# Block 0 of a fused S4D and feed-forward kernel: VectorE's limit over four steps from 7.5 to 7.0

## The chip, the cores and the metric

The kernel runs on one core of one Trainium2 chip. The metric is the device time of one execution in microseconds (us); lower is better. Each core has TensorE (PE, with its weight loads PEld), VectorE (DVE), ScalarE (ACT), GpSimd (POOL) and SyncE (SP), each with its own instruction stream in a fixed order, and 16 DMA engines that serve the queues of SP, ACT and POOL.

## What is computed

One residual layer on 2048 tokens of 576 channels: a layer norm with modulation, a state space model as a long convolution (S4D), a second layer norm, and a feed-forward network of 4608 hidden units.

```python
def _A_ref(u, log_A_real, A_imag, C_real, C_imag, log_dt, D_skip):
    ...
    P = jnp.exp((A * dt[:, None])[:, :, None] * pos[None, None, :])
    K = 2.0 * jnp.einsum("dn,dnl->dl", C, P).real
    ...  # y = causal convolution of u with K, by FFT
    return y + u * D_skip[None, None, :]

def _B_ref(x, w1, w2):
    h = jnp.einsum("bsd,df->bsf", x, w1)
    return jnp.einsum("bsf,fd->bsd", jnp.maximum(h, 0), w2)

x = A_u
sa, ca, ga, sb, cb, gb = ...  # from silu(c) @ w_mod
h = _layernorm(x) * (1 + ca) + sa
x = x + ga * _A_ref(h, ...)
h = _layernorm(x) * (1 + cb) + sb
x = x + gb * _B_ref(h, B_w1, B_w2)
```

All is float32. Where a product is large, a factor is split into a high and a low part that TensorE takes in its faster float32 form, and three products are added (high by high, high by low, low by high).

## The kernel before

**Blocks and groups.** The tokens are cut into four blocks of 512. The feed-forward network of a block runs over 36 groups g of 128 hidden units, so groups 0 to 35 are block 0 and group 36 is the first of block 1. A group has an up-projection `first(g)`, 14 products into `hps` (line L1352), here called F0, F1 and so on, and a down-projection `second(g)`, 14 products into the accumulators `acc` (L1378), here S0, S1 and so on. The code emits F(g+1) ahead of S(g). Between them ScalarE writes the high part `hh` of the rectified result (L1357) and VectorE the low part `hl` (L1358), which needs `hh`; S(g) has nine products with `hh` and five with `hl`.

**Weights.** In block 0 each group's weights are loaded from HBM by SP into `r` (`r1` has two buffers, L1297; `r2` three, L1301), ScalarE rounds them to the high part in `w` (L1317 and L1327), and VectorE subtracts to get the low part (L1322; L1333 and L1334). These subtractions are the last readers of `r`, so a load into that buffer is released by VectorE. The low parts are stored (L1434) for the later blocks, which load them instead.

**What is handed out.** While a block's groups run, the work that the next block needs is handed out in small pieces by a generator: for block 0 this is `block0()`. It holds, in this order: the rest of the convolution's kernel (rotations on VectorE, L462 to L468, and small products `kps`, L496, of TensorE); the first norm of block 1's tokens (L893 to L928); and `conv(1)`, the convolution of block 1. That one has Fourier products `ps_f` (L844) with ScalarE's copies (L845), butterflies on VectorE (L858 to L872), multiplications of spectra of 128x1152 (L1038 to L1044), inverse products `ps_i` (L1065) which VectorE adds to the tokens (L1070), and at its end the activations of block 1: norm statistics (L893, L902, L906, L907, and L903 on ScalarE), scaled tokens `h` (L1166), transposes `ps_t` through one PSUM buffer (L1174), `xf` and its high part `xh` or `xs` on ScalarE (L1178, L1180), and the low part `xl` or `xs` on VectorE (L1183, L1185). F36 needs all of `xs`, `xh` and `xl`.

After S35 ScalarE copies the accumulators (`o`, `oT`, L1462 and L1467), a product `ps_o` (L1482) turns one of them, VectorE scales them and adds them to the tokens (L1487 to L1495), and POOL stores them (L1497). Then block 1 begins with six more rotations, for which POOL loads `W`, `Zr` and `W2r`; their buffers take the place of those of `conv(1)` and of block 0's results.

**The hand-out.** `step(g)` is called four times a group, 144 times a block. Each call draws pieces from the generator. A piece yields its estimated VectorE time in us, or None for a piece of TensorE's. A call stops when the work done has reached a target that grows by 2.15 per step in block 0, when this call has 2.7 us of VectorE's work or two pieces of TensorE's, or when VectorE's work over this call and the three before it reaches a limit, `room`. A piece can also yield -1, which ends the call. What is left after step 143 is emitted at once.

A list scheduler then orders each engine's instructions: it keeps most of the code's order but puts an instruction ahead where it reckons that the one in front must wait. So a piece that is handed out at another step moves rows on all engines.

Of the kernel before, what the change touches and what calls it, by code (L numbers as in the profile page):

```python
# [24 lines left out]
NF = F // P  # L25
# [522 lines left out]
class Body:  # L548
# [736 lines left out]
    def ffn(self, gens):  # L1285
# [53 lines left out]
        def first(g):  # L1339
            xh, xl, xs = self.xT[g // NF]  # L1340
            w = w1.pop(g)
            ps = self.fps.tile([P, 512], F32, tag="hps", bufs=2, name="hps")
            ops = [(w[:, 0, 4], xs), (w[:, 1, 4], xs)]
            if g:
                for k in range(4):
                    ops += [(w[:, 0, k], xh[:, k]), (w[:, 0, k], xl[:, k]), (w[:, 1, k], xh[:, k])]
            else:
                for k in range(4):
                    ops[2 * k : 2 * k] = [(w[:, 0, k], xh[:, k]), (w[:, 1, k], xh[:, k])]
                ops += [(w[:, 0, k], xl[:, k]) for k in range(4)]  # L1350
            for i, (a, x) in enumerate(ops):
                nc.tensor.matmul(ps, a, x, start=(i == 0), stop=(i == 13))  # L1352
                if i == 6:
                    step(g)
            hh = ff.tile([P, 512], F32R, tag="hh", bufs=2, name="hh")
            hl = ff.tile([P, 512], F32R, tag="hl", bufs=2, name="hl")
            nc.scalar.activation(hh, ps, AF.Relu)  # L1357
            nc.vector.scalar_tensor_tensor(hl, ps, 0.0, hh, op0=ALU.max, op1=ALU.subtract)  # L1358
            return hh, hl

        def second(g, hh, hl):
            f = g % NF
            if f == 0:
                self.acc = [
                    self.fps.tile([P, 512], F32, tag=f"acc{i}", name=f"acc{i}_{g}")
                    for i in range(5)
                ]
            acc, w = self.acc, w2.pop(g)
            tail = [(4, w[:, 512:640], hh), (4, w[:, 512:640], hl)]
            ops = []  # L1370
            for i in range(4):
                tk = slice(i * P, (i + 1) * P)
                ops += [(i, hh[:, tk], w[:, 0:512]), (i, hh[:, tk], w[:, 640:]), (i, hl[:, tk], w[:, 0:512])]
            ops = tail + ops if f == NF - 1 else ops + tail
            seen = [0] * 5
            for j, (i, a, x) in enumerate(ops):
                seen[i] += 1
                nc.tensor.matmul(  # L1378
                    acc[i], a, x,
                    start=(f == 0 and seen[i] == 1),  # L1380
                    stop=(f == NF - 1 and seen[i] == (3 if i < 4 else 2)),
                )
                if j == 6:
                    step(g)

        done, recent = [0.0], []

        def step(g):

            at[0] += 1  # L1390
            target = self.rate(g // NF) * (at[0] % 144 or 144)
            gen = gens[g // NF]
            v = pe = 0.0
            room = (7.5, 7.0, 7.0, 7.0)[g // NF] - sum(recent[-3:])
            recent.append(0.0)
            while done[0] < target and v < min(room, 2.7) and pe < 2:
                w = next(gen, 0)
                if gen.gi_frame is None or w == -1:
                    return
                if w is None:  # L1400
                    pe += 1
                    done[0] += (0.35, 0.7, 0.7, 0.7)[g // NF]
                else:
                    v += w
                    recent[-1] = v
                    done[0] += w
# [20 lines left out]
        for g in range(n + 1):  # L1427
            if g < n:
                if g + 3 < n:
                    load_r1(g + 3)  # L1430
                if g + 3 < n:
                    load_r2(g + 3)
                for dst, src in late:
                    nc.sync.dma_start(out=dst, in_=src.bitcast(F32))  # L1434
                late.clear()
                new = (g, *first(g))
                if g + 1 < n:
                    hi2(g + 1)
                    lo2(g + 1)
                if g + 2 < n:  # L1440
                    hi1(g + 2)
                    lo1(g + 2)
                if g + 3 < n:
                    low1(g + 3)
                step(g)
            if prev is not None:
                second(*prev)
                if prev[0] % NF == NF - 1:
                    self.evacuate(prev[0] // NF)
            if g < n:  # L1450
                prev = new
                step(g)
                if g % NF == NF - 1:
                    for _ in gens[g // NF]:
                        pass
                    done[0] = 0.0
# [126 lines left out]
```

## Time and profile before

| | |
|---|---|
| median of 3 runs (lowest to highest) | 1346.46 us (1346.43 to 1348.98) |
| the profiled execution's own time | 1348.05 us |
| its span, first to last instruction | 1346.3 us |
| TensorE, VectorE, ScalarE busy | 1236.1, 892.7, 496.9 us |
| mean granted TensorE clock | 0.952 |
| block 0's groups on TensorE, F0 to the end of S35 | 223.3 to 561.3 us |

All intervals in the text come from this one profiled execution. In a timeline row the columns are start and length in us, engine, line, operation, output<-inputs, shapes, count, and in brackets the engine's idle time before it with what ended it. In a row of the chain of waits they are start, length and what ran or was waited for. Products overlap, so their pitch is read from start to start. A wait that is named in the profile is put down to what came last.

### The profile page before, as it was taken

What the parts mean: (1) busy time and instruction counts of PE and PEld (TensorE: products, weight loads), DVE (VectorE), ACT (ScalarE), POOL (GpSimd) and SP (SyncE); (2) the same over time, 40 slices, a digit from 0 to 9 for tenths busy, and PEclk for the clock granted to TensorE, in tenths of its full rate; (3) what the DMA queues carried; (4) which work ended last, traced back from release to release, by engine and by line L of the source; (5) the groups of instructions that cost most, each with busy time, mean ns of one, the idle gap of its engine ahead of it and who ended that gap; (6) DMA issues with size and microseconds to landing.
All of it is one profiled execution on the core that took longest, in us unless ns stands there. A gap on an engine that the chain in (4) does not pass through costs nothing.

```text
span 1346.3 us, 26017 instructions
## 1 busy us (share of the span) xinstructions
PE 1236.1 (92%) x10720; PEld 983.0 (73%) x10720; DVE 892.7 (66%) x1324; ACT 496.9 (37%) x863; POOL 162.5 (12%) x260
## 2 busy tenths in 40 slices
PE   4566686899999998999999999999999999999997
PEld 2345564678777786777777887887888888888885
DVE  5889988899996899588458995457996221111112
ACT  5678523222223422622244225433323352323331
POOL 0657511011000100110001000100000000000000
PEclk9558788999999999999999999999999999999998
DMA  8557983889778976797778995877996567666651
GB/s 269 217 208 298 313 317 94 313 302 328 282 252 317 334 248 238 258 400 282 243 274 328 353 355 162 268 224 267 351 394 188 176 178 230 194 197 196 201 177 53
DMA packets 120843, 345.85 MB, mean 257 GB/s; under 512 B 23916, under 2 KB 24212, under 8 KB 109972
## 3 DMA queue, kind: packets, MB, share of 16 engines
q1 hardware_dynamic: 103828, 226.96, 51.1%
q0 software_dynamic: 16384, 115.85, 22.7%
q8 instruction: 84, 1.38, 0.4%
q10 hardware_dynamic: 512, 1.38, 0.3%
q14 instruction: 35, 0.29, 0.1%
HBM read 262.73 MB, written 81.40 MB: 256 GB/s over the span
## 4 chain that ended last, share of the span: by engine, by line
PE 82%; DVE 10%; DMA 3%; issue 2%; ACT 1%; POOL 1%; POOLq 0%; ACTq 0%; SPq 0%; DVEq 0%
PE acc L1378 32%; PE hps L1352 32%; PE kps L496 5%; PE ps_f L844 5%; PE kps L71 2%; PE ps_i L1065 2%; PE ph L71 2%; DMA r<-in_w_dram 2%; DVE W1r L464 1%; DVE T L62 1%; DVE T L462 1%; DMA Zr<-Zd 1%; DVE k L62 1%; PE ps_t L1174 1%; POOL W L68 1%
## 5 line engine op out<-in xcount | busy, mean ns | idle before, releaser
L1352 PE MATMUL hps<-xh,w 128*128 128x512 f32 x1152 | 388.2, 397 | 1.2 <-ACT xh L47 1.2
L1378 PE MATMUL acc<-w,hh 128*128 128x512 f32 x1152 | 368.0, 402 | 8.0 <-ACT hh L1357 8.0
L1358 DVE SCALAR_TENSOR_TENSOR hl<-hps,hh 128x512 fp32r<-128x512 f32 x144 | 99.0, 688 | 307.2 <-ACT hh L1357 306.4
L1378 PEld LDWEIGHTS acc<-w,hh 128*128 128x128 f32 x1152 | 216.7, 189 | 55.9 <-ACT hh L1357 9.3
L1352 PEld LDWEIGHTS hps<-xh,w 128*128 128x128 f32 x1152 | 215.4, 188 | 48.6 <-ACT xh L47 2.5
L1352 PE MATMUL hps<-xl,w 128*128 128x512 f32 x576 | 231.6, 402 | 0.7 <-DVE xl L47 0.5
L1378 PE MATMUL acc<-w,hl 128*128 128x512 f32 x576 | 224.9, 402 | 2.2 <-DVE hl L1358 2.2
L1357 ACT ACTIVATE hh<-hps 128x512 fp32r<-128x512 f32 x144 | 86.0, 598 | 296.1 <-PE hps L1352 291.7
L1327 ACT ACTIVATE w<-r 128x576 fp32r<-128x576 f32 x141 | 96.7, 686 | 240.9 <-PE acc L1378 233.6
L1378 PEld LDWEIGHTS acc<-w,hl 128*128 128x128 f32 x576 | 108.0, 189 | 26.6 <-DVE hl L1358 3.5
L1317 ACT ACTIVATE w<-r 128x640 fp32r<-128x640 f32 x140 | 102.6, 733 | 65.3 <-DMA r<-in_w_dram 57.0
L1352 PEld LDWEIGHTS hps<-xl,w 128*128 128x128 f32 x576 | 108.3, 188 | 25.1 <-DVE xl L47 1.7
L1352 PE MATMUL hps<-xs,w 128*128 128x512 f32 x288 | 96.7, 409 | 1.1 <-DVE w L1322 1.1
L71 PE MATMUL kps<-W,W 128*32 128x16 f32 x2304 | 45.1, 218 | 45.9 <-POOL W L68 28.6
L496 PEld LDWEIGHTS kps<-W1r,W2r 128*32 128x32 f32 x3456 | 67.8, 146 | 24.8 <-issue 15.2
L71 PEld LDWEIGHTS kps<-W,W 128*32 128x32 f32 x2304 | 40.4, 150 | 58.3 <-POOL W L68 31.1
L1044 DVE TENSOR_TENSOR Y<-Y,T 128x1152 f32<-128x1152 f32 x60 | 79.4, 1350 | 0.0
L496 PE MATMUL kps<-W1r,W2r 128*32 128x48 f32 (+2 forms) x3456 | 76.3, 238 | 1.9 <-PE hps L1352 1.0
L845 ACT ACTIVATE Z<-ps_f 128x288 f32<-128x288 f32 x120 | 48.9, 409 | 66.2 <-PE ps_f L844 64.9
L1497 POOL DMA_DIRECT2D out_dram<-x x16 | 8.7, 545 | 471.5 <-DVE x L1489 468.9
L1352 PEld LDWEIGHTS hps<-xs,w 128*128 128x128 f32 x288 | 53.4, 189 | 12.7 <-DVE w L1322 1.5
L1378 PE MATMUL acc<-hl,w 128*128 128x512 f32 x144 | 56.6, 393 | 0.0
(230 smaller groups left out, 1568.7 us busy)
## 6 DMA issues: line engine op xcount, KB each, us to landing
r<-in_w_dram SPq DMA_DIRECT2D x144, 320.0 KB, 6.6
r<-in_w_dram SPq DMA_DIRECT2D x144, 288.0 KB, 3.7
w<-L1d SPq DMA_DIRECT2D x108, 320.0 KB, 3.2
w<-L2d SPq DMA_DIRECT2D x108, 288.0 KB, 2.7
W2r<-W2d POOLq DMA_DIRECT2D x18, 1536.0 KB, 8.8
W2d<-W SPq DMA_DIRECT2D x12, 1536.0 KB, 8.6
Ua<-Ud POOLq DMA_DIRECT2D x15, 1152.0 KB, 9.5
W<-W1d POOLq DMA_DIRECT2D x18, 768.0 KB, 10.4
```

The source lines that it names most:

```text
L62: self.tc.keep_in_program_order(self.nc.vector.tensor_tensor(out, a, b, op=op))
L71: self.tc.keep_in_program_order(self.nc.tensor.matmul(*args, **kw))
L496: nc.tensor.matmul(ps[32 * dd : 32 * dd + 32, q, :], W2[:, r, :, ch], W1[:, :, r, ch], start=(r == 0), stop=(r == 1),)
L844: nc.tensor.matmul(o, fc[:, n2, c, :], src(n2), start=True, stop=True)
L845: ev = nc.scalar.activation(Z[:, n2, c], ps[:, :PC], AF.Copy)
L1044: v(y, y, T, op=op or ALU.add)
L1317: copy(g - 1)(w1[g][:, 0], r1[g], AF.Copy)
L1327: copy(g)(w[:, 0:D], r2[g], AF.Copy)
L1352: nc.tensor.matmul(ps, a, x, start=(i == 0), stop=(i == 13))
L1357: nc.scalar.activation(hh, ps, AF.Relu)
L1358: nc.vector.scalar_tensor_tensor(hl, ps, 0.0, hh, op0=ALU.max, op1=ALU.subtract)
L1378: nc.tensor.matmul(acc[i], a, x, start=(f == 0 and seen[i] == 1), stop=(f == NF - 1 and seen[i] == (3 if i < 4 else 2)),)
```

## The change

One number, in `step` inside `ffn`:

```diff
-            room = (7.5, 7.0, 7.0, 7.0)[g // NF] - sum(recent[-3:])
+            room = (7.0, 7.0, 7.0, 7.0)[g // NF] - sum(recent[-3:])
```

In block 0 the four-step window of VectorE's handed-out work closes 0.5 earlier. With 7.5 the hand-out follows the target over most of the block and has given out all by step 135; steps 136 to 143 draw nothing but waiting pieces. With 7.0 the window binds nearly everywhere, the work falls behind the target, and the last piece, the fifth transposed tile of block 1, is drawn at step 143. No instruction's kind, count or shape changes.

Three places show the move. First TensorE, where the last inverse product of block 1 stands. Before, it is followed by F34 (`w_6106`), a group and more before the block's last down-projection:

```order
L1065 MATMUL ps_i<-V_1_6107,gc 128x288 x2
L1352 MATMUL hps<-xs_2822,w_6106 128x512 x2
L1352 MATMUL hps<-xh_2820,w_6106 128x512
L1065 MATMUL ps_i<-V_1_6107,gc 128x288 x2
L1352 MATMUL hps<-xl_2821,w_6106 128x512
L1352 MATMUL hps<-xh_2820,w_6106 128x512 x2
L1352 MATMUL hps<-xl_2821,w_6106 128x512
```

After, it is the row of `ps_i` here, three products into S35 (`w_6265`), of which eleven are left:

```order
L1378 MATMUL acc_0_3039<-hh,w_6265 128x512
L1378 MATMUL acc_0_3039<-hl,w_6265 128x512
L1378 MATMUL acc_0_3035<-w_6265,hh 128x512
L1065 MATMUL ps_i<-V_1_6181,gc 128x288 x2
L1378 MATMUL acc_0_3035<-w_6265,hh 128x512
L1378 MATMUL acc_0_3035<-w_6265,hl 128x512
L1378 MATMUL acc_0_3036<-w_6265,hh 128x512 x2
L1378 MATMUL acc_0_3036<-w_6265,hl 128x512
```

The inverse product has moved from the front of F34 into the last down-projection of the block.

Second TensorE, where block 1's transposes stand. Before, they lie among products of S34 (`w_6270`) and F36 (`w_6276`), with S35 (`w_6357`) still to come:

```order
L1378 MATMUL acc_0_3040<-hh,w_6270 128x512
L1174 MATMUL ps_t<-ident,h_6248 128x128 x2
L1174 MATMUL ps_t<-ident,h_6249 128x128 x2
L1378 MATMUL acc_0_3040<-hl,w_6270 128x512
L1352 MATMUL hps<-xs_6153,w_6276 128x512 x2
L1352 MATMUL hps<-xh_6151,w_6276 128x512
L1174 MATMUL ps_t<-ident,h_6248 128x128 x2
L1174 MATMUL ps_t<-ident,h_6249 128x128 x2
L1352 MATMUL hps<-xl_6152,w_6276 128x512
L1352 MATMUL hps<-xh_6151,w_6276 128x512 x2
L1352 MATMUL hps<-xl_6152,w_6276 128x512
```

After, S35 is over when the first transposes come, and the products of F36 (`w_6202`) and F37 (`w_6270`) are mixed behind them; the remaining transposes stand between those:

```order
L1378 MATMUL acc_0_3038<-w_6265,hh 128x512 x2
L1378 MATMUL acc_0_3038<-w_6265,hl 128x512
L1174 MATMUL ps_t<-ident,h_6340 128x128 x2
L1174 MATMUL ps_t<-ident,h_6341 128x128 x2
L1174 MATMUL ps_t<-ident,h_6340 128x128 x2
L1174 MATMUL ps_t<-ident,h_6341 128x128 x2
L1352 MATMUL hps<-xs_6246,w_6202 128x512 x2
L1352 MATMUL hps<-xs_6246,w_6270 128x512 x2
L1174 MATMUL ps_t<-ident,h_6340 128x128 x2
L1174 MATMUL ps_t<-ident,h_6341 128x128 x2
L1352 MATMUL hps<-xh_6244,w_6202 128x512
```

All five tiles' transposes have moved behind S35, so no product of block 0 is left to run beside them.

Third VectorE, the multiplications of block 1's last spectrum with its second pair of factors, from one `hl` to the next. Before, seven of them lie between the `hl` of groups 30 and 31, and the eighth behind it:

```order
L1358 SCALAR_TENSOR_TENSOR hl<-hps,hh 128x512
L1042 TENSOR_TENSOR T<-Ka,Ua 128x1152
L1333 TENSOR_TENSOR w_6045<-r_5896,w_6045 128x64
L1044 TENSOR_TENSOR Y_1_5972<-Y_1_5972,T 128x4x288
L1334 TENSOR_TENSOR w_6045<-r_5896,w_6045 128x512
L1322 TENSOR_TENSOR w_5996<-r_5957,w_5996 128x640
L1042 TENSOR_TENSOR T<-Ka,Ua 128x1152 x2
L1044 TENSOR_TENSOR Y_1_5972<-Y_1_5972,T 128x4x288 x2
L1042 TENSOR_TENSOR T<-Ka,Ua 128x1152
L1358 SCALAR_TENSOR_TENSOR hl<-hps,hh 128x512
```

After, the gap between `hl` of group 32 and of group 33 holds eight of them:

```order
L1358 SCALAR_TENSOR_TENSOR hl<-hps,hh 128x512
L1042 TENSOR_TENSOR T<-Ka,Ua 128x1152 x2
L1044 TENSOR_TENSOR Y_1_6050<-Y_1_6050,T 128x4x288
L1333 TENSOR_TENSOR w_6139<-r_5988,w_6139 128x64
L1334 TENSOR_TENSOR w_6139<-r_5988,w_6139 128x512
L1322 TENSOR_TENSOR w_6091<-r_6057,w_6091 128x640
L1044 TENSOR_TENSOR Y_1_6050<-Y_1_6050,T 128x4x288
L1042 TENSOR_TENSOR T<-Ka,Ua 128x1152 x2
L1044 TENSOR_TENSOR Y_1_6050<-Y_1_6050,T 128x4x288 x2
L1358 SCALAR_TENSOR_TENSOR hl<-hps,hh 128x512
```

They stand two groups later and all eight in one gap. Further up, the two butterflies that stand together between the `hl` of groups 27 and 28 before (L858 to L872, twice over) are spread over the gaps after 27, 28 and 29.

## The prediction

> **What bounds the kernel now.** I read the page's first row, then the stretch from block 0's first up-projection (223.29 us) to block 1's second (562.11 us), then TensorE's waits up to 592 us, where block 1 has settled. In the second fence the columns after the length are busy time and count for PE, PEld, DVE, ACT and POOL, then granted clock, DMA share and GB/s; rows of waits give sum, times, longest.
>
> ```profile
> PE 1236.1 (92%) x10720; PEld 983.0 (73%) x10720; DVE 892.7 (66%) x1324; ACT 496.9 (37%) x863; POOL 162.5 (12%) x260
> ```
>
> ```profile
> 223.29:562.11 338.82, 326.92 (x3451) 254.89 (x3451) 297.19 (x401) 110.55 (x205) 27.86 (x50) 0.99 0.79 283
> ```
>
> ```profile
> PE acc L1378 <- ACT hh L1357: 8.0, 3, 4.3
> PE acc L1378 <- DVE hl L1358: 2.2, 1, 2.2
> PE hps L1352 <- DVE w L1322: 1.1, 1, 1.1
> PE kps L496 <- PE hps L1352: 1.0, 1, 1.0
> PE kps L496 <- DVE W1r L468: 0.5, 1, 0.5
> ```
>
> TensorE is busy for 326.9 of 338.8 us there and VectorE for 297.2, so block 0 is TensorE's, with VectorE close behind. The change moves no work out of the block, and neither engine gets a shorter instruction. So all it can do to the time is to remove TensorE's waits (12.8 us in these five rows) and the slow clock behind them, or to add new ones. Two rows of the chain of waits give the scale, 14 products in 3.17 us (0.227 us each), so 6.35 us for a group of 28:
>
> ```profile
> 465.69 3.17 PE hps L1352 x14
> 468.86 3.17 PE acc L1378 x14
> ```
>
> The clock is low after such waits. In these rows the granted clock is the number before the last two: 4 us at 0.66 and at 0.57 lose 1.4 and 1.7 us, and the last two rows, at 0.87 and 0.70, lose 0.5 and 1.2 us.
>
> ```profile
> 254.00:258.00 4.00, 4.00 (x128) 3.42 (x125) 0.45 (x1) 0.49 (x1) 0.00 (x0) 0.66 0.74 271
> 519.00:523.00 4.00, 4.00 (x12) 3.09 (x12) 4.00 (x4) 1.00 (x2) 0.00 (x0) 0.57 0.83 304
> 578.00:582.00 4.00, 1.78 (x7) 1.13 (x6) 4.00 (x5) 1.22 (x2) 0.53 (x1) 0.87 1.00 406
> 582.00:586.00 4.00, 4.00 (x14) 3.24 (x13) 3.97 (x4) 0.44 (x1) 0.00 (x0) 0.70 1.06 417
> ```
>
> **The change, term by term.** The limit over four steps falls by 0.5, and the hand-out of block 0 ends at step 143, the last, where it now ends at step 135.
>
> *The hand-over to block 1 (cost).* Block 1's activations (norm, transposes, xh and xl) are the last thing handed out. Now they are done two groups ahead, beside products of block 0. In the new order the last inverse product ps_i stands only 11 products before the end of S35 (the down-projection of group 35), and all transposes stand behind it. The chain is timed from its rows now, the timeline of PE, DVE and ACT:
>
> ```profile
> 538.61 1.24 PE L1065 MATMUL ps_i<-V,gc 128*128 128x288 f32 x4
> 539.89 0.46 DVE L1070 TENSOR_TENSOR x<-ps_i,x 128x288 f32<-128x288 f32 x1
> 542.98 4.47 ACT L1166 ACTIVATE h<-x,mv 128x576 f32<-128x576 f32 x8
> 552.63 0.78 ACT L1178 ACTIVATE xf<-ps_t,m_sb,m_cb 128x512 f32<-128x512 f32 x1
> 554.15 0.78 ACT L1178 ACTIVATE xf<-ps_t,m_sb,m_cb 128x512 f32<-128x512 f32 x1
> 557.39 0.69 DVE L1185 TENSOR_TENSOR xl<-xf,xh 128x512 fp32r<-128x512 f32 x1 [0.64 <-ACT xh L1180]
> 553.46 0.66 PE L1174 MATMUL ps_t<-ident,h 128*128 128x128 f32 x4
> 553.87 0.48 PE L1378 MATMUL acc<-hl,w 128*128 128x512 f32 x1
> 561.30 1.00 PE L1482 MATMUL ps_o<-ident,o 128*128 128x64 f32 x8
> ```
>
> From 538.61 to 558.08 it takes 19.5 us: ScalarE scales for 4.47 us, then serves five tiles 1.5 us apart or more. It does about as much other work between in the new order (four copies of the accumulators, one weight tile) as now. TensorE has for those 19.5 us: the ps_i itself 0.9, 11 products 2.5, five times four transposes at 0.41 (553.46 to 553.87), 2.05, the 16 products of F36 and F37 that stand before the last xl, 3.6, and ps_o 0.8. That is 9.9 us. A wait of **9.6 us** is left, 7 to 12.
>
> *VectorE late before it (cost).* In the new order the multiplications that are left for block 1's last spectrum fall into one gap: between hl of group 32 and hl of 33 are eight of them and three weight subtractions, priced by these rows of VectorE's timeline.
>
> ```profile
> 497.69 0.21 DVE L1333 TENSOR_TENSOR w<-r,w 128x64 fp32r<-128x64 f32 x1
> 497.83 0.69 DVE L1334 TENSOR_TENSOR w<-r,w 128x512 fp32r<-128x512 f32 x1
> 498.43 0.82 DVE L1322 TENSOR_TENSOR w<-r,w 128x640 fp32r<-128x640 f32 x1
> 506.54 2.62 DVE L1038 TENSOR_TENSOR Y<-K,Ua 128x1152 f32<-128x1152 f32 x2
> ```
>
> Two large ones take 2.62 us with an overlap of 0.1, so 1.27 each, the three subtractions 1.48 from start to start, and hl itself about 0.6: 12.2 us against TensorE's 6.35. By the same pitches the seven gaps from hl of 26 on hold 7.1, 7.8, 4.2, 10.4, 4.8, 8.0 and 12.2 us, while TensorE takes 6.35 to 7.3 for a group with its ps_i. Carried forward, never below zero, VectorE is some 3 us late before the last gap and 9 behind it; the order of S33 (nine hh products ahead of hl's five) covers about 7: **+2.3**, 1 to 6. In S34 and S35 hl's are by the same count 0.6 and 0.8 us late, **+1.4**. One slow clock behind these waits is **+1.4**, as at 254 us.
>
> The Trainium skill (TensorE: Matmul & The Clock Gate, What's actually happening) has the clock halved only after an idle window of about 3.4 us. The rows at 578 us show 0.87 and 0.70 behind a wait of 2.2 us, so here the trace disagrees and decides. By the page the late hl would cost no clock and the sum would be 1.4 us lower.
>
> *The wait at 514 us (gain).* Now hl of group 28 comes late behind two whole butterflies, the weight load behind it goes out late, into four transfers of POOL's queue, and ScalarE waits for it ahead of hh:
>
> ```profile
> 503.78 11.88 DMA r<-in_w_dram
> 516.89 0.74 ACT L1317 ACTIVATE w<-r 128x640 fp32r<-128x640 f32 x1 [7.09 <-DMA r<-in_w_dram]
> 518.74 1.44 PE L1378 MATMUL acc<-w,hh 128*128 128x512 f32 x4 [4.35 <-ACT hh L1357]
> 528.23 0.50 PE L1352 MATMUL hps<-xs,w 128*128 128x512 f32 x1 [1.08 <-DVE w L1322]
> ```
>
> 4.35, 1.08 and the clock's 1.7 are 7.1 us. The new order splits those butterflies over groups 27 to 29, so hl comes in time; the same transfers still meet a weight load. With a latency of 9 to 12 us it would be 3 to 6 us late for ScalarE, of which TensorE's lead takes about half. I take **−7.1 + 3.0**; ends −7.1 and 0.
>
> *The start (gain).* Groups 1 and 2 wait twice for hh behind the same kind of load:
>
> ```profile
> 242.18 0.74 ACT L1317 ACTIVATE w<-r 128x640 fp32r<-128x640 f32 x1 [8.19 <-DMA r<-in_w_dram]
> 244.02 0.96 PE L1378 MATMUL acc<-w,hh 128*128 128x512 f32 x3 [2.09 <-ACT hh L1357]
> 252.77 0.82 PE L1378 MATMUL acc<-w,hh 128*128 128x512 f32 x2 [1.60 <-ACT hh L1357]
> ```
>
> The new order runs all of F3 ahead of S2, which covers the first wait; the weight subtraction that frees the next load stands some 1.7 us earlier. Of 3.7 us of waits and 1.4 of clock about 2.8 stay: **−2.3**, ends −5 and 0. The two kps rows above, 1.5 us and some pauses, go with a VectorE that is asked for less: **−1.7**, ends −1.7 and +2.
>
> *The start of block 1 (gain).* Now VectorE stands in a rotation that waits for Zr, with hl queued behind it:
>
> ```profile
> 576.83 1.76 DVE L462 TENSOR_TENSOR T<-W,Zr 128x1536 f32<-128x1536 f32 x1 [9.92 <-DMA Zr<-Zd]
> 580.92 0.80 PE L1378 MATMUL acc<-w,hl 128*128 128x512 f32 x1 [2.22 <-DVE hl L1358]
> ```
>
> In the new order block 0's results leave VectorE before hl of group 36, where now they follow it, so Zr is asked for a group (6.35 us) earlier against the products. 2.2 us and the clock's 1.7 go: **−3.9**, ends −3.9 and 0.
>
> ScalarE, SP and POOL issue what they did; the transfers are the same ones, moved later with their producers. They cost nothing more as long as TensorE has products in hand; where it has none, that is the terms above.
>
> Sum: 9.6 + 2.3 + 1.4 + 1.4 − 7.1 + 3.0 − 2.3 − 1.7 − 3.9 = +2.7 us on a profiled execution of 1348.05 us (span 1346.3). The runs' median is 1346.46, 1.6 below it; on that the forecast is **1349.1 us**. A change within 0.2% (2.7 us) can't be told from none here, so this one lies on the border of slower.
>
> **Rivals.**
> *Faster.* The bubble at the hand-over stays near its lower end and the two weight-load waits go whole: 7 + 1 + 0.7 + 1 − 7.1 − 5 − 1.7 − 3.9 = −8.0, so 1338.5; half of that, 1342.5, with the bubble at 9.6 and late hl's cheap. It decides from about 7 us of waits removed beyond block 1's 3.9. For it: VectorE's 5 us gaps in groups 34 and 35 are idle room, and the loads are late because VectorE is. Against: those gaps are what covers the hand-over. The Trainium skill (Perfetto Trace Analysis, Optimization Strategy) holds that interleaving stretches with different limits may improve a kernel, which speaks for this case; no run here shows it yet.
> *Clearly slower.* The loads collide again, now with a VectorE that has its multiplications in one heap: the wait at 514 us only moves (0 for −7.1 + 3.0), the start gives nothing back, and late hl's cost 5 for 2.3: 9.6 + 5 + 1.4 + 1.4 − 1.7 − 3.9 = +11.8, 1358.3. It needs one 12 us load in the group whose hl is late.
> *No effect.* TensorE's work binds and every wait has its like in the other order: 1346.5.
>
> **How the numbers follow.** Forecast (−1 to +6 us, 1345.5 to 1352.5) 0.45, clearly slower 0.22, faster 0.20, no effect 0.13. Half of the forecast's case lies above 2.7 us: slower 0.43, same 0.35 (the rest of it less a little, and no effect), faster 0.22. The range leaves out the far part of both outer cases: 1341.5 to 1357.5.
>
> **What would show it.** Right: between the end of S35 and the first products of block 1 TensorE waits for ScalarE (xf, xh) some 9 us in sum; the five waits above shrink; no wait of 2 us for hl behind Zr. Wrong: TensorE busy through the hand-over, or a new wait for hh over 4 us behind a weight load around groups 30 to 34, or kps waits in groups 4 to 18.

## The result, and the profile after

The changed kernel takes 1356.71 us (median of 4 runs, 1355.21 to 1359.66) where the kernel before takes 1346.94 (4 runs): a ratio of 1.0066, with a 95% interval of 1.0044 to 1.0089. By this ratio it is slower by about 9 us (the medians are 9.8 us apart); the prediction said 1349.1, which is 2.7 us more than before, with "slower" as the likeliest of the three signs. The profiled execution took 1355.62 us with a span of 1353.8, 7.5 us longer than the one shown of before.

First the page's row of engines and its row of the queue that brings TensorE its instructions (packets, MB, share); then the stretch from block 0's first up-projection to block 1's second, with the columns as in the prediction.

```profile
PE 1240.3 (92%) x10720; PEld 987.4 (73%) x10720; DVE 893.5 (66%) x1324; ACT 496.9 (37%) x863; POOL 162.0 (12%) x260
q8 instruction: 84, 1.38, 0.4%
```

```profile
223.29:570.51 347.22, 331.41 (x3454) 259.45 (x3454) 300.35 (x405) 110.16 (x203) 27.76 (x50) 0.98 0.78 276
```

The stretch is 347.2 us long for 338.8. The queue's row will matter below: 84 packets for 10720 products and as many weight loads, so one packet of 16 KB holds about 128 products with their loads. (An experiment below that has 100 products more shows 85.) TensorE's waits from 223.29 to 592 us (sum, times, longest) are another set than before:

```profile
PE acc L1378 <- ACT hh L1357: 4.7, 1, 4.7
PE hps L1352 <- issue: 3.3, 2, 1.7
PE acc L1378 <- DVE hl L1358: 3.2, 2, 1.7
PE ps_t L1174 <- ACT h L1166: 2.9, 4, 0.8
PE ps_t L1174 <- ACT xf L1178: 1.3, 2, 0.9
PE hps L1352 <- DVE xs L1183: 0.8, 1, 0.8
```

Gone is the wait for hh at 514 us. New are the chain of block 1's activations (h, xf, xs) and a row without a producer ("issue"). The chain as it now runs, in the timelines of PE, DVE and ACT:

```profile
551.24 1.14 PE L1065 MATMUL ps_i<-V,gc 128*128 128x288 f32 x4
554.25 4.45 ACT L1166 ACTIVATE h<-x,mv 128x576 f32<-128x576 f32 x8
555.49 0.33 PE L1174 MATMUL ps_t<-ident,h 128*128 128x128 f32 x1 [0.59 <-ACT h L1166]
558.76 0.47 PE L1174 MATMUL ps_t<-ident,h 128*128 128x128 f32 x1 [0.76 <-ACT h L1166]
562.03 2.07 PE L1352 MATMUL hps<-xs,w 128*128 128x512 f32 x4 [0.81 <-DVE xs L1183]
569.53 0.69 DVE L1185 TENSOR_TENSOR xl<-xf,xh 128x512 fp32r<-128x512 f32 x1 [0.23 <-ACT xh L1180]
```

and the clock there (the number before the last two of each row):

```profile
552.00:556.00 4.00, 3.23 (x14) 2.18 (x12) 2.67 (x16) 2.53 (x7) 0.00 (x0) 1.00 0.92 307
556.00:560.00 4.00, 1.13 (x3) 0.46 (x3) 0.00 (x0) 4.00 (x9) 0.00 (x0) 0.75 0.37 136
560.00:564.00 4.00, 3.08 (x9) 2.19 (x10) 3.37 (x6) 3.81 (x8) 0.00 (x0) 0.50 0.28 74
564.00:568.00 4.00, 3.61 (x20) 2.71 (x19) 3.00 (x6) 2.81 (x4) 0.00 (x0) 0.89 0.00 0
```

From the ps_i at 551.24 to the end of the last xl at 570.22 the chain takes 19.0 us, and TensorE has too little for it: 1.13 us busy out of 4, then half a clock. At their pitch in the kernel before, its products in these 19.0 us are 10.1 us of work (an estimate), which leaves 8.9 us. The waits for h, xf and xs are 4.9 us of that; about 4 us are products that take longer at the lower clock.

The table below shows where the time goes. At each moment of the kernel before I take the work that TensorE has done (its products, each at its mean pitch in that trace) and look when another kernel has done the same; that is its lag. Each column is how much the lag grows over a stage, in us, from one profiled execution of each kernel, so differences under 1 us mean little. The kernels below the first row are the experiments; products that an experiment adds don't count as work. Four of them reach the first column late, by 8.0 us (after_s50), 5.0 (before_s50 and before_i50) and 2.6 (after_i50), which is told there. The executions of e_tail_fast, after_i50 and before_i50 are the slowest of 12, some 5 us above their medians. Of the 2.5 us of e_tail_slow in the first column 1.8 are a wait at 267 us of the kind that is told under "The first half".

| kernel | start, 223–268 | kps products, 268–509 | middle, 509–530 | late hl, 530–541 | hand-over, 541–574 | block 1's start, 574–603 | sum |
|---|---|---|---|---|---|---|---|
| changed | +2.3 | +2.6 | −7.3 | +1.8 | +8.5 | −0.4 | +7.5 |
| e_tail_slow | +2.5 | −1.0 | −5.8 | −0.6 | +2.5 | −0.8 | −3.2 |
| e_first48 | +1.9 | +6.9 | +0.8 | +1.2 | 0.0 | −0.2 | +10.4 |
| e_last70 | +0.6 | +1.5 | −5.4 | −0.4 | +0.7 | +3.0 | 0.0 |
| m9 | −0.2 | +0.5 | −1.3 | 0.0 | 0.0 | 0.0 | −1.1 |
| e_tail_fast | +2.4 | +2.5 | −7.3 | +2.7 | +9.2 | +0.7 | +10.2 |
| e_start | +0.7 | +8.4 | +0.2 | 0.0 | 0.0 | +0.4 | +9.7 |
| u4 | +0.5 | −0.5 | −6.1 | −0.6 | +1.5 | +2.7 | −2.4 |
| before_i50 | −0.1 | +6.2 | −1.3 | 0.0 | 0.0 | +0.7 | +5.5 |
| after_i50 | +1.7 | +0.9 | −7.3 | +2.5 | +8.7 | +0.9 | +7.4 |
| before_s50 | −0.9 | +3.7 | −1.4 | 0.0 | 0.0 | +2.3 | +3.8 |
| after_s50 | +1.1 | +1.9 | −7.4 | +3.3 | +8.5 | +0.5 | +8.0 |

### The profile page after: what moved, and what is told of

Read it like the earlier page. It is cut to its first block, busy times and chain, and to the rows that moved or that the text cites. A ratio compares the mean times of both kernels' runs of the same rounds, so it can differ in the third digit from the quotient of the medians.

```text
span 1353.8 us, 26012 instructions
## 1 busy us (share of the span) xinstructions
PE 1240.3 (92%) x10720; PEld 987.4 (73%) x10720; DVE 893.5 (66%) x1324; ACT 496.9 (37%) x863; POOL 162.0 (12%) x260
## 4 chain that ended last, share of the span: by engine, by line
PE 80%; DVE 9%; DMA 3%; issue 3%; ACT 2%; POOL 1%; ACTq 0%; POOLq 0%; SPq 0%; DVEq 0%
PE hps L1352 31%; PE acc L1378 31%; PE kps L496 5%; PE ps_f L844 5%; PE kps L71 2%; PE ph L71 2%; DMA r<-in_w_dram 2%; PE ps_i L1065 2%; DVE T L62 1%; DMA Zr<-Zd 1%; DVE k L62 1%; DVE Y L1044 1%; POOL W L68 1%; PE ps_t L1174 1%; DVE W L62 1%
## 5 line engine op out<-in xcount | busy, mean ns | idle before, releaser
L1044 DVE TENSOR_TENSOR Y<-Y,T 128x1152 f32<-128x1152 f32 x60 | 79.5, 1348 | 0.0
```

The lines of the kernel that those rows point to most:

```text
L1044: v(y, y, T, op=op or ALU.add)
```

## The experiments

After the result my theory was: the hand-over costs 8.5 us, the wait at 514 us gives 7 back, and the rest of the loss (about 5 us by 510 us) is the new order of block 0's first half. The rival was that this first-half loss belongs to one execution, or that the hand-over is not where the loss is made. Each edit below is in the one line that sets the limit, or is shown. `at[0]` counts the steps of block 0, four in a group. All ratios are to runs of the kernel before on the same chip, where its median was 1347.8 to 1349.0; one execution of it lies anywhere from 1343.8 to 1353.9 there.

### Halves of the change

**e_tail_slow**, the old limit up to step 119, then a lower one, so that the hand-out ends as late as in the changed kernel:

```diff
-            room = (7.5, 7.0, 7.0, 7.0)[g // NF] - sum(recent[-3:])
+            room = ((7.5 if at[0] < 120 else 4.5) if g < NF else 7.0) - sum(recent[-3:])
```

> Block 0's limit stays 7.5 up to step 119, as in the kernel before, and is 4.5 from there, so that the hand-out ends at step 143 as in the changed kernel. The first 29 groups keep the order of before, the two butterflies between hl of group 26 and of 28 too, so the wait for hh at about 514 us should stay (4 us and a slow clock). Theory (the late end of the hand-out opens a wait at the hand-over that nothing covers; 8.7 us in the changed kernel): here four of the five transposed tiles stand behind S35, so 6 to 9 us of waits for ScalarE between S35 and group 37, time before +6 to +9, 1352.5 to 1355.5. Rival (the end costs little, and the changed kernel's loss is spread over its first half): within 2.5 us of before.

Measured: 1344.44 us, ratio 0.9974 (0.9957 to 0.9991), faster than before. The theory was wrong twice: the hand-over costs 2.5 us, not 6 to 9, and the wait at 514 us does not stay as it was (1.7 us are left). The rival, within 2.5 us of before, missed as well.

**e_first48**, the changed kernel's limit up to step 71 and then a higher one, so that the end of block 0 is that of before:

```diff
+            room = ((7.0 if at[0] < 72 else 8.5) if g < NF else 7.0) - sum(recent[-3:])
```

> Block 0's limit is 7.0 up to step 71, as in the changed kernel, and 8.5 from there, so that the hand-out ends at step 135 as in the kernel before, with TensorE's order of before from group 33 on; the two butterflies between hl of group 26 and of 28 are split over two gaps. Theory (in the changed kernel's first half the new order costs about 5 us up to 510 us: 2 at the start, the rest at waits that no producer ends, and the wait at 514 us is worth 5 to 8): +5 at 510 us, -5 to -8 in the middle, 0 at the hand-over, so -3 to 0 against before, 1343.5 to 1346.5. Rival (the 5 us of the first half belong to one execution and not to the order): -5 to -8, 1339 to 1341.5.

Measured: 1357.28, ratio 1.0065 (1.0041 to 1.0088): as slow as the whole change, without any cost at the hand-over. The time lies far above both forecasts. The first half alone is enough for the loss; the rival fell, and so did the gain in the middle.

**e_last70**, the old limit up to step 71, the new one behind:

```diff
+            room = ((7.5 if at[0] < 72 else 7.0) if g < NF else 7.0) - sum(recent[-3:])
```

> Block 0's limit is 7.5 up to step 71, as in the kernel before, and 7.0 from there, as in the changed kernel; the hand-out ends at step 137, two later than before and six earlier than in the changed kernel. The butterflies stay together in one gap. Theory (the hand-over pays by how late the hand-out ends: first transposed tiles among S34, the last ones behind S35): 2 to 5 us of waits for ScalarE at the hand-over, the wait at 514 us stays, so +2 to +5, 1348.5 to 1351.5. Rival (it only costs when nothing is left to cover it, and two steps are covered): within 1.5 us of before.

Measured: 1347.96, ratio 0.9993 (0.9976 to 1.0010). The rival was right in the time and at the hand-over (0.7 us), but again the wait at 514 us shrank, by 5.4 us, and block 1's start took 3 back.

So the second half of the change, run by itself, is no loss, and the first half by itself is as slow as all of it. Three things needed explaining: the hand-over, 514 us, and the first half.

**The hand-over** goes by the number of products between the last inverse product and the end of S35: 11 in the changed kernel (+8.5), 29 in e_tail_slow (+2.5), 39 in u4 (+1.5), 43 in e_last70 (+0.7), and nothing in the kernels that keep before's end. (e_tail_fast, with 23, is told below; it lost more than these numbers would give.) From 11 to 29 that is 18 products of 0.227 us, 4.1 us, and four transposes that come earlier; measured 6.0. In the changed kernel what the chain costs is its length less the work behind its first link: 8.9 us by the count above, for 8.5 in the table.

### The wait at 514 us

**m9** keeps the order of before except for the two butterflies ahead of hl of group 28, which it splits over two gaps, as the change does:

```diff
+            room = ((7.5 if at[0] < 77 else 7.0 if 97 <= at[0] < 122 else 8.5) if g < NF else 7.0) - sum(recent[-3:])
```

> Block 0's limit is 7.5 up to step 76, 7.0 from step 97 to 121 and 8.5 at the other steps, so that the order of before stays up to about group 25 and again from group 28 on, with the hand-out ending at step 135; only the two butterflies between hl of group 26 and of 28 are split over two gaps, as the changed kernel splits them. Theory (hl of group 28 is late behind both butterflies, and so is the load behind it, hence the wait for hh at 514 us): the wait goes, -4 to -7 us, 1339.5 to 1342.5, faster than both kernels. Rival (the transfers of POOL's queue meet a weight load anyway and the wait only moves): -1 to +1.

Measured: 1346.18, ratio 0.9984 (0.9969 to 0.9999). The wait is still there, 3.3 us at 517.16, as the rival had it, and the time is 2.2 us below before by the ratio, a little more than the rival's 1 us and less than the theory's 4 to 7. So the butterflies, on which the prediction put it, are not its main cause. What is, stands in VectorE's timeline behind hl of group 30, first of before, then of e_tail_slow:

```profile
511.61 0.68 DVE L1358 SCALAR_TENSOR_TENSOR hl<-hps,hh 128x512 fp32r<-128x512 f32 x1
514.39 1.36 DVE L1042 TENSOR_TENSOR T<-Ka,Ua 128x1152 f32<-128x1152 f32 x1 [2.10 <-DMA Ua<-Ud]
517.68 0.82 DVE L1322 TENSOR_TENSOR w<-r,w 128x640 fp32r<-128x640 f32 x1
```

```profile
511.56 0.68 DVE L1358 SCALAR_TENSOR_TENSOR hl<-hps,hh 128x512 fp32r<-128x512 f32 x1
512.89 0.81 DVE L1322 TENSOR_TENSOR w<-r,w 128x640 fp32r<-128x640 f32 x1
514.65 2.62 DVE L1042 TENSOR_TENSOR T<-Ka,Ua 128x1152 f32<-128x1152 f32 x2 [0.94 <-DMA Ua<-Ud]
```

In before the multiplication that waits for Ua stands ahead of the subtraction of L1322, which F32 needs from its second product on; TensorE's order there has one product of F32 ahead of the wait for hh. In e_tail_slow the subtraction comes first, 4.8 us earlier, and all 14 products of F32 run ahead of the wait, which falls from 4.35 us to the 1.71 of this row:

```profile
518.99 1.20 PE L1378 MATMUL acc<-w,hh 128*128 128x512 f32 x4 [1.71 <-ACT hh L1357]
```

The load of 12 us that ends the wait is the same in both (ScalarE's rounding starts at 516.89 and at 517.14). In the four other kernels that I read for it the rule holds: L1322 behind multiplications in m9 (3.3 us), e_start (4.3) and e_first48 (5.6; there behind those of L1038 and L1044, which wait for no load there), ahead of them in e_last70 (1.3).

### The first half

The three kernels with the changed order of the first half lose at the same places, and the waits there have no producer. Their places are best told by how many products stand before them, which is the count of a window that ends just there; the changed kernel's two, with their rows in PE's timeline:

```profile
302.62 0.62 PE L1352 MATMUL hps<-xh,w 128*128 128x512 f32 x2 [1.74 <-issue]
391.49 0.39 PE L1352 MATMUL hps<-xh,w 128*128 128x512 f32 x1 [1.58 <-issue]
```

```profile
0.00:302.60 302.60, 211.35 (x3789) 161.60 (x3790) 257.52 (x454) 148.82 (x241) 101.78 (x154) 0.80 0.71 257
0.00:391.48 391.48, 298.64 (x5194) 231.09 (x5195) 337.62 (x538) 170.42 (x280) 110.74 (x171) 0.84 0.74 266
```

3789 and 5194 products. e_first48 waits behind 3789, 5194 and 5705. The remainders by 128 are 77, 74 and 73, and 128 products are one packet of the instruction queue. So the new theory: TensorE stands where one block of its instructions ends and the next has not come. Four runs test it. Two make nothing but 25 (50) more calls of a product at 33 us, where TensorE is idle; on every engine all else is in the same order, and everything behind stands 50 (100) products further on:

```diff
-        for nm in ps:
+        for nm in [*ps] + ["sa"] * 1:   # * 2 in after_s100
```

**after_s50** and **after_s100**, on the changed kernel:

> The changed kernel with 25 more calls of a product at about 33 us (block 0's mps_sa is worked out twice; 50 products in the records, about 2.2 us in a place where TensorE is idle for 4.8). Nothing else moves on any engine, but every later product stands 50 further on in TensorE's instruction stream. Theory (the waits of TensorE that no producer ends, the rows 'hps <- issue' and 'kps <- issue', come from fetching its instructions, and fall where a block of the stream ends at the wrong moment): the three waits at 302, 391 and 594 us, 5.2 us in sum, move or go, while the waits that end with ACT or DVE stay where they are; the time then lies anywhere from -5 to +3 against the changed kernel, ratio to before 1.003 to 1.009. Rival (they belong to the order of the products): they stand at the same products within 0.3 us, ratio 1.006 to 1.008.

> The same with 50 more calls (100 products in the records, about 4.4 us in the idle 4.8). Theory: the three waits without a producer move again, to other products than with 25 calls; waits for ACT and DVE stay; ratio to before 1.002 to 1.010. Rival: same places as in the changed kernel, ratio 1.006 to 1.009.

Measured: 1361.89, ratio 1.0099 (1.0074 to 1.0123), and 1364.70, 1.0124 (1.0102 to 1.0145). The waits at 302 and 391 us are gone in both: from 260 us on the first has no such wait up to 405 us, the second none up to 500. From 268 to 404 us, over both places, the changed kernel's lag to before grows by 1.4 us; here it grows by 0.3 and falls by 0.4. The third wait, at 594 us, stays at its product (1.65, 1.65 and 1.64 us in the three traces): the theory was wrong to count it. It starts again just as a rotation of VectorE ends (L466, 593.56 and 0.95 long), and is that one's. The times came out slower than expected, and that is ahead of block 0: its first product starts at 231.3 and 234.4 us, in the changed kernel at 223.3, since more such waits came up in the stretch before it (their rows there sum to 22.7 and 24.7 us, for 17.1).

**before_s50**, the 25 calls on the kernel before:

> The kernel before with the same 25 more calls at about 33 us. Theory (instruction fetch): in block 0, where the kernel before has a wait without a producer of 0.4 us only, one to three of 1.5 to 2.5 us appear, so +1 to +5 against before, ratio 1.001 to 1.004. Rival (the order of before has none of them, wherever its stream begins): rows of issue in block 0 stay under 1 us and the time within 1 us of before.

Measured: 1355.31, ratio 1.0054 (1.0033 to 1.0076). The kernel before, which had 0.4 us of such waits in block 0, gets 3.0 us from 260 to 450 us, the largest behind 5705 products; the rest of its loss is again ahead of block 0, whose first product starts 5.0 us later. Nothing but the place in the stream was changed.

The pair of after_s50 and before_s50 tells what the change costs with 50 products more ahead of block 0: the medians are 6.6 us apart, and the two ratios put together give about 1.0045 (1.001 to 1.008). In their traces 3.1 us of the difference lie ahead of block 0.

**e_tail_fast**, the changed kernel up to step 119, then faster:

```diff
+            room = ((7.0 if at[0] < 120 else 9.0) if g < NF else 7.0) - sum(recent[-3:])
```

> Block 0's limit is 7.0 up to step 119, as in the changed kernel, and 9.0 from there: the hand-out ends at step 140 for 143, and 23 products stand between the last inverse product and the end of S35, where the changed kernel has 11. Theory (the wait at the hand-over is the chain from the last inverse product to xl, less the products behind it; 8.7 us with 11 of them, about 2.5 with 29, none with 43): 4 to 5 us at the hand-over, so about 4 less than the changed kernel, ratio to before 1.002 to 1.005. Rival (the loss lies in the first half and the hand-over only passes it on): ratio 1.006 to 1.007, as the changed kernel.

Measured: 1354.73, ratio 1.0045 (1.0030 to 1.0059), which is within the theory's range; but the interval overlaps that of the changed kernel, and the trace doesn't show the saving. Its profiled execution, the slowest of its 12, waits 2.6 us for h, xf and xs and runs at a clock of 0.55 and 0.60 behind that, and it waits 4.7 us for weight subtractions (L1334) to which VectorE comes late, at 536 and 548 us. The lag still grows by 9.2 us over the hand-over. About 2.3 us of that are waits for VectorE ahead of the last inverse product (1.45 for the second subtraction, 0.82 for V); some 6.6 remain for the chain, where the theory had 4 to 5. The waits of the first half are again behind 3789 and 5194 products.

**after_i50** and **before_i50** put 25 calls into the idle time ahead of the last inverse products before block 0, so that everything earlier stays as it was:

```diff
                 v(xv(n2, p), pv, xv(n2, p), op=ALU.add)
                 yield 0.45
+                for _ in range(25 if s == 0 and p == 0 and n2 == tiles[-1] else 0):
+                    nc.tensor.matmul(
+                        ps[:, PC : PC + 16], self.gc[:, 0, 0, :], V[:, 0, 0][:, :16],
+                        start=True, stop=True,
+                    )
```

> The changed kernel with 25 calls of a small product (16 columns, into unused columns of an inverse product's tile) ahead of the last inverse products before block 0, where TensorE is idle for 7.5 us (202 to 210 us). Nothing else moves; what runs before 202 us is untouched, and from there every product stands 50 further on in TensorE's stream, as in the run with the 25 calls at 33 us. Theory (a wait comes where the count of products passes a certain place in each block of 128, if TensorE is not covered there): no waits at 302 and 391 us (3.5 us less), one of about 1 us at product 5705 (425 us), so -1 to -3.5 against the changed kernel: 1.004 to 1.006. Rival (the extra products cost by themselves, as the runs with them at 33 us came out slower): +3 to +8 against the changed kernel, 1.009 to 1.012.

> The kernel before with the same 25 calls at the same place. Theory: waits without a producer come at products 3406, 5705 and 6597, as in the run of before with the calls at 33 us, 3 to 5.5 us in sum, and the stretch ahead of 202 us costs nothing: +3 to +5.5 against before, ratio 1.002 to 1.004; the changed kernel is then slower than this one by 0 to 4 us, for 8 without the calls. Rival (the extra products cost by themselves): +5 to +8 with no waits at those products; or nothing at all, within 1 us of before.

Measured: 1353.44, ratio 1.0040 (1.0027 to 1.0054), and 1352.89, ratio 1.0037 (1.0020 to 1.0053). The added products took 9.0 and 9.18 us and not the 6 that were free, which delays the next inverse product by 2.6 and 2.8 us (the gap of 7.86 us ahead of it becomes 10.48 and 10.66). The trace of before_i50 reaches block 0 another 2.2 us later; most of that it lost ahead of the added products. Even with that the changed kernel came to the lower end of what the theory expected, and is about 3 us faster with the added products than without (ratios of 1.0040 and 1.0066, whose intervals overlap), which no cost of theirs would make it. It waits 0.72 us behind 5705 products, where the theory had about 1. The kernel before waits behind 3406, 5705 and 6597 products, as expected; the first two (in these two kernels every line behind L1071 has a number 5 higher):

```profile
275.11 0.41 PE L496 MATMUL kps<-W1r,W2r 128*32 128x16 f32 x6 [1.48 <-issue]
418.64 0.66 PE L496 MATMUL kps<-W1r,W2r 128*32 128x16 f32 x24 [3.05 <-issue]
```

```profile
0.00:418.63 418.63, 329.33 (x5705) 257.03 (x5706) 362.76 (x582) 176.06 (x293) 112.46 (x173) 0.84 0.74 264
```

This execution is the slowest of its 12, and shows more than their median (1352.89 less the 2.8 of delay is 2.3 above its before). What matters is the pair: with the added products here the change costs 0.5 us of 1353, and the two ratios put together give about 1.0003, from 0.998 to 1.0025. Without them it is 1.0066, and with as many products added at 33 us about 1.0045. So what the change costs depends on where its stream stands, and not on the count of products alone.

**e_start** has the new limit for the first 12 steps only:

```diff
+            room = ((7.0 if at[0] < 12 else 7.5) if g < NF else 7.0) - sum(recent[-3:])
```

> Block 0's limit is 7.0 up to step 11 and 7.5 from there: groups 1 to 4 run in the changed kernel's order (all of F3 ahead of S2), the middle and the end in the order of before. Theory (the load behind ScalarE's wait lands when the queues let it, not by when it is asked for, and the products of F3 are only run earlier): one wait of 4.5 to 5.5 us for hh in place of 2.1 and 1.6, +1 to +2.5 by 270 us, the rest as before but for waits without a producer (0 to 4): ratio 1.001 to 1.004. Rival (the new order of the start is neutral or a gain): -2 to +0.5, 0.9985 to 1.0004.

Measured: 1355.87, ratio 1.0056 (1.0035 to 1.0078). More than either theory allowed, and not at the start: up to 268 us it loses 0.7. Then come two waits behind 3789 and 4683 products, the first where the changed kernel has one too, and a smaller one behind 4300:

```profile
299.87 0.92 PE L496 MATMUL kps<-W1r,W2r 128*32 128x16 f32 x41 [2.63 <-issue]
357.50 0.45 PE L496 MATMUL kps<-W1r,W2r 128*32 128x16 f32 x13 [2.36 <-issue]
```

```profile
0.00:357.49 357.49, 260.99 (x4683) 200.23 (x4684) 307.44 (x504) 161.34 (x264) 108.45 (x166) 0.85 0.73 260
299.00:303.00 4.00, 3.13 (x46) 2.63 (x46) 4.00 (x5) 0.87 (x2) 1.05 (x2) 0.64 0.91 344
```

The last row shows the clock at 0.64 behind the first wait, so that such a place costs about 4 us (an estimate: 4 us at 0.64 lose 1.4) and not 2.6. The lag grows by 8.4 us over these three places, as much as the whole change costs, from another order of the first groups.

### A version that keeps the gains

**u4** has a low limit only from step 120 to 129:

```diff
+            room = ((7.5 if at[0] < 120 else 5.0 if at[0] < 130 else 8.5) if g < NF else 7.0) - sum(recent[-3:])
```

> Block 0's limit is 7.5 up to step 119, 5.0 to step 129, 8.5 from there; the hand-out ends at step 138, and 39 products stand between the last inverse product and the end of S35. Up to hl of group 29 the order is that of before; behind it the weight subtractions stand ahead of the multiplication that waits for Ua, as in the run with 4.5. Theory (the wait at 514 us is that multiplication's, which holds the subtraction that F30 needs; and 39 products cover the hand-over): 514 us costs 2 for 4.4, the rest of the middle as in the run with 4.5, hand-over under 1 us: -4 to -7 against before, 1340 to 1343 on the first runs' level, ratio 0.995 to 0.997. Rival (the new order's waits at block 1's start, for the rotations, take it back, as 7 us in the run with 7.0 from step 72): within 1.5 us of before.

Measured: 1345.88, ratio 0.9984 (0.9967 to 1.0001). That lies between the theory and the rival. The middle gives 6.1 us, as the theory had it, and the hand-over costs 1.5, where it had under 1; then the rival's wait takes 2.7 back, behind the first rotations of block 1, beside a wait behind 6596 products:

```profile
583.33 0.28 PE L496 MATMUL kps<-W1r,W2r 128*32 128x32 f32 x2 [3.34 <-issue]
591.37 0.44 PE L496 MATMUL kps<-W1r,W2r 128*32 128x32 f32 x10 [1.45 <-issue]
```

By the ratio it is 0.16% below before, and the interval reaches 1. The best of all versions is e_tail_slow, 0.26% below before.

## Why the prediction was right, and where it was not

The time lies in the range and the sign was the likeliest, but in the sum (+2.7) three terms had the wrong size or sign (the start, the kps rows, block 1's start), one had the wrong reason (514 us), and one loss was in no term. The sum came to +7.5 us in the trace; the median lies 0.8 us below the upper end of the range and nearer to the rival "clearly slower" than to the forecast. So the sign was right, and the time was in the range by its width more than by the sum.

- *Hand-over*, forecast 9.6 (7 to 12): 8.5 over its stage. Right in mechanism and size, shown by the changed kernel's chain (19.0 us for 19.5, TensorE's work in it 10.1 for 9.9) and by its shrinking as more products follow the last inverse product. The sign that was to show it, "some 9 us in sum" of waits, came only by half: the waits are 4.9 us, the rest is the low clock behind them. It alone doesn't decide the sign: e_first48 has none of it and is as slow, with less gained in the middle.
- *Late hl*, 2.3 + 1.4, and 1.4 for the clock: 1.8 over its stage. There is one wait of 1.67 us at 539.91, and S34 and S35 have none. The clock stays at full speed behind it:

```profile
538.00:542.00 4.00, 2.33 (x11) 1.72 (x10) 4.00 (x7) 1.54 (x4) 0.00 (x0) 1.00 0.51 166
```

- *The wait at 514 us*, −7.1 + 3.0: −7.3. The low end of the term was the answer, and the reason was wrong. I put it on the late hl and on a load that meets POOL's transfers; m9 and e_tail_slow show that it is the order of a subtraction and a multiplication that waits for Ua, which decides how many products of F32 TensorE has to run meanwhile. In the changed kernel a later load is late too (ScalarE waits 9.48 us for it, until 525.12), but L1322 stands ahead of the multiplications there and TensorE doesn't wait.
- *The start*, −2.3: +2.3, and +0.7 to +2.4 in the four experiments with that order. The step that failed is "the weight subtraction that frees the next load stands some 1.7 us earlier". It does, but the load lands no earlier: SP issues it at 240.63 us for 242.26, and ScalarE gets it at 251.72 for 251.50. Running F3 ahead only joins the two waits of 2.09 and 1.60 us into one of 4.72, at the end of which the clock is down for longer:

```profile
252.99 3.35 PE L1378 MATMUL acc<-w,hh 128*128 128x512 f32 x7 [4.72 <-ACT hh L1357]
252.00:256.00 4.00, 3.01 (x7) 2.43 (x8) 4.00 (x5) 2.25 (x4) 0.00 (x0) 0.50 0.63 246
```

- *The kps rows*, −1.7 (−1.7 to +2): +2.6. They did go; in their place stand the two waits at ends of instruction blocks, 3.3 us, which no term knew.
- *Block 1's start*, −3.9 (−3.9 to 0): −0.4, the other end. The step that failed is that an earlier Zr sets TensorE free. (Of the clock's 1.7 us in that term, 0.5 was read from a row in which TensorE is busy for 1.78 of 4 us, and can't all be a loss.) VectorE still stands for it, and hl behind it, and when hl is in time, the next products wait for the rotation instead:

```profile
583.82 1.76 DVE L462 TENSOR_TENSOR T<-W,Zr 128x1536 f32<-128x1536 f32 x1 [9.20 <-DMA Zr<-Zd]
587.90 0.50 PE L1378 MATMUL acc<-w,hl 128*128 128x512 f32 x1 [1.50 <-DVE hl L1358]
594.61 0.28 PE L496 MATMUL kps<-W1r,W2r 128*32 128x32 f32 x2 [1.65 <-issue]
```

- *The clock.* The prediction weighed the Trainium skill (TensorE: Matmul & The Clock Gate, What's actually happening), by which only an idle window of about 3.4 us halves the clock, against the 2.2 us of before, and let the trace decide. Of the new waits, those of 1.58 to 1.74 us leave the clock at 1.00, as the Trainium skill has it; behind 2.63 us it is 0.64, where the Trainium skill would have it whole. For the late hl the Trainium skill gave the better sum. The length of a wait is not all: the 50 products of 16 columns in before_i50, behind a wait of 1.24 us, ran at 0.60 of the clock from 207 to 211 us and then at half of it, though TensorE is shown as busy throughout:

```profile
211.00:215.00 4.00, 4.00 (x21) 4.00 (x20) 3.13 (x7) 0.00 (x0) 0.00 (x0) 0.50 0.07 31
```

As to the rivals: "the loads collide again" did not happen at 514 us, though its time (1358.3) was the nearest, and no rival named what decides between "same" and "slower". Of the signs of being wrong, a wait for hh over 4 us did come, but in group 2 (4.72 us) and not around groups 30 to 34.

The terms that belong to the order (start, middle, late hl, hand-over, block 1) sum to +4.9 us in the changed kernel's trace, and the stage of the kps products adds 2.6. With 50 products more in the stream the first are about as large: +6.0 in after_s50 less before_s50, +7.2 in after_i50 less before_i50. But the stage of the kps products then gives 1.8 and 5.3 back, since there it is the kernel before that stands at the ends of blocks. So the part of the order costs 5 to 7 us at all three places, in single executions, and what the whole change costs goes with the ends of blocks: 0.66% at its own place, about 0.45% with the products at 33 us (with part of it ahead of block 0), and nothing that can be measured with the products at 202 us.

Against the sum of +2.7, the start, the kps rows and block 1's start came out 12.4 us worse, and 514 us, the late hl and the hand-over 7.6 us better. That the errors cancel for the most part is luck; the 4.8 us that remain are within the range.

What stays open: why a packet comes late at one end of a block and not at another has been read from the records only, not varied by itself; why the two pairs with 50 products more are 6.6 and 0.5 us apart, though the count is the same through block 0; and the loss of e_first48 from 404 to 431 us (3.8 us) is only in part its wait behind 5705 products.

## What to carry to other kernels

When TensorE's stream holds runs of very short products, a reordering moves the places where its instruction blocks end against those runs, and here that alone was worth about as much as the change (before_s50 is 0.54% slower than before with the same order): before you believe a gain or a loss under 1%, run both kernels again with some idle products added ahead of the stretch, at more than one place. Read "issue" waits by the count of products before them; if the counts agree by 128, this is the likely cause. And what a hand-over costs is the chain's length less the work that is left behind its first link, so count those products first; and look at what stands between a late transfer's user and the subtraction or copy that the next group needs.

## What the runs showed of the hardware

- In the 14 traces, 280 ends of blocks fall between 260 and 430 us, 20 in each (product counts 3278, 3406, 3534 and so on by 128, sliding by one in about four blocks). From the start of one product to the start of the next it takes 0.7 to 3.3 us at 20 of them. At 19 of the 20 the instruction packet's record starts 2.2 to 2.6 us before TensorE goes on, and at all 20 the 100 products before took 2.3 to 4.0 us, two runs of 48 kps products mostly. Of the 112 other ends behind as short a run at most five have a packet that started less than 2.25 us before, and over 70 have one that started 3 us or more before. This fits some 2.3 us from the packet's start until TensorE can go on, and a run of short products that uses up a block faster than that.
- Waits at such counts sum to 15 to 25 us ahead of block 0 in every trace here, 17 in that of before. There two rows of PE's timeline show 128 products of 16 columns in 2.1 us, each behind a wait without a producer; the first lies behind 2007 products, the second behind 2388, and the next such waits follow 128 products later:

```profile
142.42 2.14 PE L71 MATMUL kps<-W,W 128*32 128x16 f32 x128 [3.05 <-issue]
167.85 2.15 PE L71 MATMUL kps<-W,W 128*32 128x16 f32 x128 [3.91 <-issue]
```

- A load into a released buffer was asked for earlier and landed at the same moment (ScalarE's rounding starts at 251.50 and 251.72 us): that fits a landing that is set by what else the DMA engines have to do (the DMA share from 248 to 252 us is 1.03 in the changed kernel), from one pair of loads.
- 50 products of 16 columns took 9.18 us, 0.18 each, with a weight load of 128 columns for each, at a clock of 0.60 and 0.50; the same width in the first of the kps rows above, with 32 columns of weights, takes 0.017, at a clock of 0.50.
